# Preparing expert weights piece by piece between the steps of a two-layer mixture-of-experts stage

## The chip, the cores and the metric

The kernel runs on one core of one Trainium2 chip. The metric is the device time of one launch in microseconds, the median of the runs shown. Engines are named as in the profile: PE (TensorE), DVE (VectorE), ACT (ScalarE), POOL (GpSimd) and SP (SyncE, whose queue issues the loads).

## What is computed

Attention with a threshold, a gated MLP, and a soft mixture of eight experts, all in float32. The change touches the last part only:

```
logits = x @ w_gate                          # x: 2304 x 512, 8 experts
P = exp(logits - logits.max())
for _ in range(8):                           # Sinkhorn
    P /= P.sum(1, keepdims=True) + 1e-09
    P /= P.sum(0, keepdims=True) + 1e-09
    P *= N / E
for e in range(E):                           # w1: 512 x 1024, w2: 1024 x 512 for each expert
    h = np.maximum(x @ w1[e], 0.0)
    out += P[:, e:e + 1] * (h @ w2[e])
```

## The kernel before

**Work.** Every float32 matrix is held as two float16 parts (a high part and the remainder), and a product takes three passes. In the last part each expert is cut into two halves of 512 hidden columns, so there are 16 half experts (`h` = 0 to 15, `NE`), and the tokens into three groups (`NGR`). A half expert and a group make a unit `u` (48 units). Within a unit a block scheme with seven products (`ORDER`, `SECOND`) replaces the eight of a 2 x 2 block product, for x·w1 (`first_step`, L894) and for h·w2 (`second_step`, L966).

**PE's order.** It is written out by hand (`manual_schedule`, L1023). The loop at L1024 goes over steps `k`; each has one first step (six matmuls of 384 columns, into the PSUM tiles `X` or `Z`; two chains of seven first steps for a unit), and after step 20 one or two second steps (six matmuls of 256 columns, into `P` or `Q`), three for every two `k`. A unit is 14 first and 21 second steps; a half expert is 42 values of `k`. `P` has two PSUM banks, `Q` one (L1003). A second step accumulates onto the bank that the last-but-one left, so DVE must have taken the earlier result out of it (L992, `acc <- P` or `acc <- Q`, called an eviction here) before PE may write again.

**The other engines.** They run in the order that the scheduler gives them from the order of tracing and from its own estimate of times. In the steady part DVE has the evictions (L992), the sums `u <- Z,u` (L922, L931, L940) and the remainders `h <- u,h` (L889 for the operands 0, 1 and 2). ACT copies and clips (L920 to L941) and makes the high parts (L888). POOL builds the four remaining operands in eight instructions a chain (L943 to L946 and L889).

**The weights of the next half expert.** `load_w` (L720) loads 1 MB into the tile `raw` (L728, names `w1r`, `w2r`), takes the largest magnitude with two reductions on DVE (`w1m`, L731) and one maximum (L735), and forms three sums and one difference on POOL (L742 to L745, L749 to L752, names `w1s`, `w2s`). `prep_w` (L755) passes the maximum through a matmul with the identity (`w1mxp`, L131) and a reduction (L133), makes a scale of it in five small DVE instructions (L78 to L84), and then splits seven blocks into high part and remainder: `split` (L715) is one ACT copy (L717) and one DVE subtraction (L718) for a block. `raw` has one buffer, shared by w1 and w2. In the loop (L1044 to L1052) `load_w` is traced at the first step of a unit and `prep_w` ten steps later, w1 in the first unit of a half expert, w2 in the second. There is nothing that holds these instructions to a place among DVE's, ACT's or POOL's others.

**Loads of x.** Tiles `xo` (`load_x`, L777) have `XB` = 12 buffers; all loads go through SP's queue in order. For the first three units they are transposing loads in three pieces and are written back (`x2s`).

Of the kernel before, what the change touches and what calls it, by code (L numbers as in the profile page):

```python
# [7 lines left out]
F32 = mybir.dt.float32  # L8
# [11 lines left out]
def kernel(  # L20
# [29 lines left out]
    P = 128  # L50
# [498 lines left out]
    def mlp_out(j, tT, pool=None):  # L549
        if pool is not None:  # L550
            xf = pool.tile([P, KD, FH], F32, tag="raw", name="xf", bufs=1)
            xf = xf.rearrange("p k f -> p (k f)").rearrange("p (o d) -> p o d", d=HD)
            xh = pool.tile([P, NOP, HD], F32, tag="sums", name="xh")
            xh = xh.rearrange("p o d -> p (o d)").bitcast(F16)
            xh = xh.rearrange("p (o l d) -> p o l d", l=2, d=HD)
# [155 lines left out]
    KX = 4  # L711
    XB = 12
    UNITS = NE * NGR
# [5 lines left out]

    def load_w(which, h):  # L720

        e, f0 = h // 2, h % 2 * FH
        if which == 1:
            src = moe2_w1[e, :, f0 : f0 + FH]
        else:
            src = moe2_w2[e, f0 : f0 + FH, :]
        r = pb.tile([P, 4, 512], F32, tag="raw", name=f"w{which}r{h}", bufs=1)
        nc.sync.dma_start(out=r, in_=src.rearrange("(k p) f -> p k f", p=P))  # L728
        m = small([P, 2], f"w{which}m", bufs=2)
        for a in range(2):  # L730
            V.tensor_reduce(  # L731
                m[:, a : a + 1], r[:, 2 * a : 2 * a + 2], AX.XY, ALU.max,
                apply_absolute_value=True,
            )
        V.tensor_tensor(m[:, 0:1], m[:, 0:1], m[:, 1:2], ALU.max)  # L735
        sm = pb.tile([P, 7, HD], F32, tag="sums", name=f"w{which}s{h}")
        sm = sm[:, 0:6].rearrange("p (o k) f -> p o k f", o=3)
        q11, q12 = r[:, 0:2, 0:HF], r[:, 0:2, HF:]
        q21, q22 = r[:, 2:4, 0:HF], r[:, 2:4, HF:]
        if which == 1:  # L740
            a11, a21, a12, a22 = q11, q12, q21, q22
            G.tensor_tensor(sm[:, 0], a21, a22, ALU.add)  # L742
            G.tensor_tensor(a21, a11, a21, ALU.subtract)
            G.tensor_tensor(sm[:, 1], sm[:, 0], a11, ALU.subtract)
            G.tensor_tensor(sm[:, 2], a12, sm[:, 1], ALU.subtract)  # L745
            parts = (a11, a12, a22, a21)
        else:
            b11, b12, b21, b22 = q11, q12, q21, q22
            G.tensor_tensor(sm[:, 0], b12, b11, ALU.subtract)  # L749
            G.tensor_tensor(b12, b22, b12, ALU.subtract)  # L750
            G.tensor_tensor(sm[:, 1], b22, sm[:, 0], ALU.subtract)
            G.tensor_tensor(sm[:, 2], b21, sm[:, 1], ALU.subtract)  # L752
            parts = (b11, b12, b22, b21)
        return m, parts, sm

    def prep_w(which, h, loaded, pool, bufs=1):

        m, parts, sm = loaded
        w = pool.tile([P, NOP, 2, 2, HF], F16, tag=f"w{which}", name=f"w{which}_{h}", bufs=bufs)
        bits = 3 if which == 1 else 8  # L760
        s, inv = pow2_scale(all_max(m[:, 0:1], f"w{which}mx"), 1, bits, f"w{which}_{h % 3}")
        for o, a in enumerate((*parts, sm[:, 0], sm[:, 1], sm[:, 2])):
            split((w[:, o, 0], w[:, o, 1]), a, s[:, 0:1])
        return w, inv

# [4 lines left out]

    w1[0], inv1[0] = prep_w(1, 0, load_w(1, 0), pb)

# [112 lines left out]
    def operand(u, op, f, src, engine):  # L885

        t = pc.tile([P, 2, TW], F16, tag="h", name=f"h{u}_{op}_{f}", bufs=26)
        A.activation(t[:, 0], src, AF.Copy)  # L888
        engine.tensor_tensor(t[:, 1], src, t[:, 0], ALU.subtract)  # L889
        hs[u, op, f] = t  # L890
# [74 lines left out]
    def second_step(u, jj, j, pools):  # L965
# [50 lines left out]

    w2[0], inv2[0] = prep_w(2, 0, load_w(2, 0), pc, 2)
    BEHIND = 7
    steps = None
    held = {}  # L1020
    owed = []
    done = 0
    with tc.manual_schedule(engines={mybir.EngineType.PE}):  # L1023
        for k, (c, j) in enumerate(ahead):  # L1024
# [4 lines left out]
            if f == 1:  # L1029
                owed.append(u * NOP + j + XB)  # L1030
            if h > 0 or (f == 0 and j == 6):
                if h == 0:
                    logits(g)
                for t in owed:
# [18 lines left out]
            want = (k + 1 - 14 - BEHIND) * 3 // 2
# [52 lines left out]
```

## Time and profile before

| | us |
|---|---|
| median of 3 runs | 2411.78 |
| lowest and highest | 2406.57, 2448.46 |
| the profiled execution's own time | 2404.14 |
| its span, first to last instruction | 2402.3 |

The profile is of one execution. A line number stands for a line of the kernel; "idle before" is time in which the engine stood before that instruction, with what released it.

### The profile page before, as it was taken

What the parts mean: (1) busy time and instruction counts of PE and PEld (TensorE: products, weight loads), DVE (VectorE), ACT (ScalarE), POOL (GpSimd) and SP (SyncE); (2) the same over time, 40 slices, a digit from 0 to 9 for tenths busy, and PEclk for the clock granted to TensorE, in tenths of its full rate; (3) what the DMA queues carried; (4) which work ended last, traced back from release to release, by engine and by line L of the source; (5) the groups of instructions that cost most, each with busy time, mean ns of one, the idle gap of its engine ahead of it and who ended that gap; (6) DMA issues with size and microseconds to landing.
All of it is one profiled execution on the core that took longest, in us unless ns stands there. A gap on an engine that the chain in (4) does not pass through costs nothing.

```text
span 2402.3 us, 44050 instructions
## 1 busy us (share of the span) xinstructions
PE 2030.8 (85%) x16464; PEld 1476.9 (61%) x16464; DVE 1652.3 (69%) x3442; ACT 1333.0 (55%) x2786; POOL 1275.2 (53%) x1404
## 2 busy tenths in 40 slices
PE   1468889999999597978889788887888878888899
PEld 0245766767766365656666566665666656666677
DVE  6998777777443567676676766667666676666756
ACT  6877878877433454444454454544545445454553
POOL 1346665667433644555555555555555555555554
PEclk9769999999999798999999899998999989999999
DMA  9885878777371642333333333333333333333332
GB/s 262 206 180 118 166 136 167 152 137 136 61 178 45 158 124 84 104 101 110 105 103 104 101 110 104 102 102 105 110 104 103 102 104 110 103 102 101 96 99 80
DMA packets 372038, 286.80 MB, mean 119 GB/s; under 512 B 286064, under 2 KB 299504, under 8 KB 371824
## 3 DMA queue, kind: packets, MB, share of 16 engines
q1 hardware_dynamic: 371232, 283.97, 45.0%
q8 instruction: 129, 2.11, 0.4%
q14 instruction: 85, 0.70, 0.1%
q0 software_dynamic: 64, 0.00, 0.0%
q10 hardware_dynamic: 528, 0.02, 0.0%
HBM read 192.04 MB, written 21.23 MB: 89 GB/s over the span
## 4 chain that ended last, share of the span: by engine, by line
PE 51%; DVE 13%; DMA 7%; issue 2%; ACT 2%; POOL 1%; SPq 0%; DVEq 0%; ACTq 0%; POOLq 0%
PE X L910 13%; PE P L982 12%; PE Q L982 10%; PE Z L910 9%; DVE w L718 4%; PE gv L530 4%; DMA w1r<-in_moe_w_dram 3%; DMA w2r<-in_moe_w_dram 3%; PE x L561 2%; DVE h L889 2%; DVE acc L992 2%; ACT w L717 1%; DVE w1m L731 1%; DVE w2m L731 1%; DMA eT<-hl 1%
## 5 line engine op out<-in xcount | busy, mean ns | idle before, releaser
L982 PEld LDWEIGHTS <-h 128*128 128x128 f16 x6048 | 607.4, 101 | 301.5 <-issue 155.9
L910 PEld LDWEIGHTS <-w 128*128 128x128 f16 x4032 | 406.2, 101 | 272.6 <-issue 88.2
L910 PE MATMUL X<-xo,w 128*128 128x384 f16 x2304 | 466.6, 342 | 53.9 <-ACT u2c L927 7.4
L982 PE MATMUL P<-w,h 128*128 128x256 f16 x3456 | 483.1, 281 | 20.5 <-DVE acc L992 13.9
L982 PE MATMUL Q<-w,h 128*128 128x256 f16 x2592 | 370.4, 282 | 115.3 <-DVE acc L992 112.8
L992 DVE SCALAR_TENSOR_TENSOR acc<-P,coef,acc 128x256 f32<-128x256 f32 x540 | 258.7, 479 | 143.7 <-PE P L982 140.9
L910 PE MATMUL Z<-xo,w 128*128 128x384 f16 x1728 | 333.2, 330 | 0.0
L992 DVE SCALAR_TENSOR_TENSOR acc<-Q,coef,acc 128x256 f32<-128x256 f32 x405 | 194.1, 479 | 149.7 <-PE Q L982 147.6
L304 POOL TENSOR_TENSOR hl<-e,hl 128x512 f16<-128x512 f32 x144 | 171.7, 1193 | 228.3 <-ACT hl L303 150.2
L530 PE MATMUL gv<-xnT,wg 128*128 128x256 f16 x1296 | 167.7, 278 | 10.2 <-DVE u L540 7.9
L530 PE MATMUL gv<-xnT,wv 128*128 128x256 f16 x1296 | 167.6, 275 | 0.0
L561 PE MATMUL x<-wo,tT 128*128 128x512 f16 x648 | 144.4, 379 | 1.1 <-DVE u L540 0.9
L330 PE MATMUL pv<-vs,eT 128*128 128x64 f16 (+1 forms) x2240 | 103.2, 201 | 49.9 <-DMA eT<-hl 45.3
L530 PEld LDWEIGHTS <-wg 128*128 128x128 f16 x1296 | 126.4, 99 | 30.1 <-issue 10.7
L330 PEld LDWEIGHTS <-eT 128*128 128x128 f16 (+1 forms) x2240 | 91.0, 106 | 76.8 <-DMA eT<-hl 59.3
L298 DVE SCALAR_TENSOR_TENSOR e<-S,nt,e 128x576 f32<-128x576 f32 x144 | 116.5, 810 | 30.8 <-ACT e L296 30.4
L530 PEld LDWEIGHTS <-wv 128*128 128x128 f16 x1296 | 126.4, 99 | 15.7 <-issue 0.2
L292 DVE TENSOR_REDUCE nt<-S 128x1 f32<-128x576 f32 x144 | 107.0, 751 | 31.2 <-PE S L282 30.6
L296 ACT ACTIVATE e<-S,nt,c 128x576 f32<-128x576 f32 x144 | 117.9, 820 | 0.3 <-issue 0.3
L545 POOL TENSOR_TENSOR tT<-u,tT 128x256 f16<-128x256 f32 x108 | 74.2, 687 | 74.6 <-ACT tT L544 74.6
L303 ACT ACTIVATE hl<-e 128x576 f16<-128x576 f32 x144 | 97.1, 676 | 17.3 <-DVE e L298 10.2
L561 PEld LDWEIGHTS <-tT 128*128 128x128 f16 x648 | 62.2, 98 | 71.8 <-issue 1.2
(2636 smaller groups left out, 3665.3 us busy)
## 6 DMA issues: line engine op xcount, KB each, us to landing
xo<-x2s SPq DMA_DIRECT2D x315, 384.0 KB, 3.0
w1r<-in_moe_w_dram SPq DMA_DIRECT2D x16, 1024.0 KB, 5.0
w2r<-in_moe_w_dram SPq DMA_DIRECT2D x16, 1024.0 KB, 5.3
x2s<-xo SPq DMA_DIRECT2D x21, 384.0 KB, 2.7
wgatew<-in_moe_w_gate_dram SPq DMA_DIRECT2D x12, 512.0 KB, 6.0
wo<-in_moe_w_out_dram SPq DMA_DIRECT2D x12, 512.0 KB, 4.2
wvalw<-in_moe_w_val_dram SPq DMA_DIRECT2D x12, 512.0 KB, 4.4
x2d<-xs SPq DMA_DIRECT2D x24, 256.0 KB, 2.5
```

The costliest lines, as they stand in the source:

```text
L292: V.tensor_reduce(mx, sv, AX.XY, ALU.max)
L296: A.activation(ev, sv, AF.Exp, bias=nt[:, 0:1], scale=st["c2"][:, c : c + 1])
L298: V.scalar_tensor_tensor(ev, sv, nt[:, 1:2], ev, ALU.is_ge, ALU.mult, accum_out=sums[:, slot : slot + 1])
L303: A.activation(hl[:, 0:S], e, AF.Copy)
L304: G.tensor_tensor(hl[:, S + REM :], e[:, 0 : NCH * P], hl[:, 0 : NCH * P], ALU.subtract)
L330: T.matmul(o, lhsT=a, rhs=r, start=n == 0, stop=n == len(mm) - 1)
L530: T.matmul(gv[:, a, :], lhsT=w[:, l, kk, f * P : (f + 1) * P], rhs=xt[:, r * KD + kk, :], start=n == 0, stop=n == 3 * KD - 1,)
L561: T.matmul(ps, lhsT=tT[f][:, l, o : o + P], rhs=wo[:, f, r, :], start=n == 0, stop=n == 3 * KF - 1,)
L718: V.scalar_tensor_tensor(dst[1], src, s, dst[0], ALU.mult, ALU.subtract)
L910: T.matmul(ps, lhsT=w[:, a, l, kk, f * P : (f + 1) * P], rhs=xb[:, r * 2 + kk, :], start=n == 0 and j in (0, 1, 3), stop=n == 5, skip_grou ...
L982: T.matmul(ps, lhsT=hs[u, ao, f][:, l, jj * P : (jj + 1) * P], rhs=w2[h][:, bo, r, f, :], start=n == 0 and j in (0, 1, 3), stop=n == 5, sk ...
L992: V.scalar_tensor_tensor(y, ps, coef[h][:, i : i + 1], y, ALU.mult, ALU.add)
```

## The change

`load_w` and `prep_w` become one generator, `weight`, that stops (`yield`) after the load, after each reduction, after the maximum, after the scale, after each of POOL's four sums and after each of the seven splits: 17 calls of `next` in all. Before the loop a table `due` gives each call a step `k`: `base` plus an entry of `AT`. For w1 of half expert `hn` the base is 42·(hn−1), for w2 it is 18 later; the first pair is 10 and 6 more late. `behind()` ties every instruction of a piece behind the instruction of the main work that was last traced on the same engine (`main`: the operand's ACT copy and its difference on DVE or POOL, and the eviction on DVE). SP has no such entry, so loads are not tied. `raw` gets a second buffer, and `XB` goes from 12 to 10 for the room. The weights of half expert 0 are both loaded and scaled before the last MLP block. During half expert 0, `load_x` may run as soon as the logits of its group are traced.

```diff
-            xf = pool.tile([P, KD, FH], F32, tag="raw", name="xf", bufs=1)
+            xf = pool.tile([P, KD, FH], F32, tag="raw", name="xf", bufs=2)
...
-    XB = 12
+    XB = 10
...
-    def load_w(which, h):
+    main = {}
+
+    @contextmanager
+    def behind():
+
+        with ExitStack() as es:
+            for ins in main.values():
+                es.enter_context(tc.issue_after(ins.ins))
+            yield
+
+    def weight(which, h, pool, bufs=1):
...
-        r = pb.tile([P, 4, 512], F32, tag="raw", name=f"w{which}r{h}", bufs=1)
+        r = pb.tile([P, 4, 512], F32, tag="raw", name=f"w{which}r{h}", bufs=2)
         nc.sync.dma_start(out=r, in_=src.rearrange("(k p) f -> p k f", p=P))
+        yield
...
+        for x in sums:
+            G.tensor_tensor(*x)
+            yield
+        w = pool().tile([P, NOP, 2, 2, HF], F16, tag=f"w{which}", name=f"w{which}_{h}", bufs=bufs)
         for o, a in enumerate((*parts, sm[:, 0], sm[:, 1], sm[:, 2])):
             split((w[:, o, 0], w[:, o, 1]), a, s[:, 0:1])
+            yield
...
+    AT = (0, 6, 7, 7, 9, 10, 11, 11, 12, 12, 13, 14, 15, 16, 17, 18, 19)
...
+    first_w2 = weight(2, 0, lambda: pc, 2)
+    for _ in range(5):
+        next(first_w2)
...
-        A.activation(t[:, 0], src, AF.Copy)
-        engine.tensor_tensor(t[:, 1], src, t[:, 0], ALU.subtract)
+        main["A"] = A.activation(t[:, 0], src, AF.Copy)
+        main[engine is V] = engine.tensor_tensor(t[:, 1], src, t[:, 0], ALU.subtract)
...
-            V.scalar_tensor_tensor(y, ps, coef[h][:, i : i + 1], y, ALU.mult, ALU.add)
+            main[True] = V.scalar_tensor_tensor(y, ps, coef[h][:, i : i + 1], y, ALU.mult, ALU.add)
...
+    due = {}
+    for hn in range(1, NE):
+        for which, base in ((1, 42 * (hn - 1) + 10 * (hn == 1)), (2, 42 * (hn - 1) + 18 + 6 * (hn == 1))):
+            n = weight(which, hn, (lambda p: lambda: p)(w1_pool(hn) if which == 1 else pc), which)
+            for x in AT:
+                due.setdefault(base + x, []).append(n)
...
-            un, hn = k // 14, k // 14 // NGR + 1
-            if hn < NE and k % 14 in (0, 10) and un % NGR < 2:
-                which = 1 + un % NGR
-                if k % 14 == 0:
-                    held[which] = load_w(which, hn)
-                elif which == 1:
-                    w1[hn], inv1[hn] = prep_w(1, hn, held[1], w1_pool(hn))
-                else:
-                    w2[hn], inv2[hn] = prep_w(2, hn, held[2], pc, 2)
+            for n in due.pop(k, ()):
+                with behind():
+                    next(n, None)
```

Three places show how the order moves. In the rows the names carry a number that grows with the order of tracing; `Z_1`, `Z_3` are Z tiles of steps 1 and 3, `Q_0_3` is the Q tile of step 3 of the first token block.

The first is DVE, the reductions of a w1 (here of half expert 7). Before, they stand right behind the last split of the w2 ahead of them:

```order
L718 SCALAR_TENSOR_TENSOR w_6_17353<-w2s_17096,w_0_s,w_6_17353 128x512
L931 TENSOR_TENSOR u33b<-Z_3_17344,u33b 128x384
L992 SCALAR_TENSOR_TENSOR acc_11683<-P_1_17424,coef,acc_11683 128x256
L731 TENSOR_REDUCE w1m<-w1r_17814 128x1
L922 TENSOR_TENSOR u34a<-Z_1_17460,u34a 128x384
L731 TENSOR_REDUCE w1m<-w1r_17814 128x1
L889 TENSOR_TENSOR h_2_1_17403<-u33b,h_2_1_17403 128x384
L992 SCALAR_TENSOR_TENSOR acc_11730<-Q_1_3_17472,coef,acc_11730 128x256
```

Now they stand five main instructions apart, and the maximum and the reduction of the identity matmul follow with one eviction between:

```order
L905 TENSOR_TENSOR h_1_0_17954<-u36d,h_1_0_17954 128x384
L739 TENSOR_REDUCE w1m<-w1r_17810 128x1
L1008 SCALAR_TENSOR_TENSOR acc_12315<-P_2_17877,coef,acc_12315 128x256
L938 TENSOR_TENSOR u37a<-Z_1_17973,u37a 128x384
L1008 SCALAR_TENSOR_TENSOR acc_12399<-P_0_17989,coef,acc_12399 128x256
L956 TENSOR_TENSOR u36c<-Z_3_17885,u36c 128x384
L1008 SCALAR_TENSOR_TENSOR acc_12399<-Q_0_1_18023,coef,acc_12399 128x256
L905 TENSOR_TENSOR h_0_1_17982<-u37a,h_0_1_17982 128x384
L739 TENSOR_REDUCE w1m<-w1r_17810 128x1
L1008 SCALAR_TENSOR_TENSOR acc_12399<-P_0_17989,coef,acc_12399 128x256
L744 TENSOR_TENSOR w1m<-w1m 128x1
L133 TENSOR_REDUCE w1mx<-w1mxp 128x1
```

In PE's order the matmul `w1mxp` now stands behind the first step that follows the second step whose result is evicted between the second reduction and L744.

The second is DVE, the splits of a w2. Before, seven splits in four runs with one eviction between the runs:

```order
L718 SCALAR_TENSOR_TENSOR w_6_17353<-w2r_17090,w_0_s,w_6_17353 128x512 x2
L992 SCALAR_TENSOR_TENSOR acc_11598<-P_0_17277,coef,acc_11598 128x256
L718 SCALAR_TENSOR_TENSOR w_6_17353<-w2r_17090,w_0_s,w_6_17353 128x512 x2
L992 SCALAR_TENSOR_TENSOR acc_11683<-P_1_17424,coef,acc_11683 128x256
L718 SCALAR_TENSOR_TENSOR w_6_17353<-w2s_17096,w_0_s,w_6_17353 128x512 x2
L992 SCALAR_TENSOR_TENSOR acc_11683<-Q_1_1_17432,coef,acc_11683 128x256
```

Now the first five of the seven (a sixth follows four rows on, the seventh after seven more):

```order
L718 SCALAR_TENSOR_TENSOR w_7_18614<-w2r_18290,w_1_s,w_7_18614 128x512
L1008 SCALAR_TENSOR_TENSOR acc_11811<-P_2_18624,coef,acc_11811 128x256
L905 TENSOR_TENSOR h_2_0_18659<-u40b,h_2_0_18659 128x384
L718 SCALAR_TENSOR_TENSOR w_7_18614<-w2r_18290,w_1_s,w_7_18614 128x512 x2
L1008 SCALAR_TENSOR_TENSOR acc_11765<-Q_2_3_18671,coef,acc_11765 128x256
L1008 SCALAR_TENSOR_TENSOR acc_11811<-P_2_18624,coef,acc_11811 128x256
L718 SCALAR_TENSOR_TENSOR w_7_18614<-w2r_18290,w_1_s,w_7_18614 128x512
L905 TENSOR_TENSOR h_1_0_18707<-u40d,h_1_0_18707 128x384
L938 TENSOR_TENSOR u41a<-Z_1_18726,u41a 128x384
L718 SCALAR_TENSOR_TENSOR w_7_18614<-w2s_18551,w_1_s,w_7_18614 128x512
L1008 SCALAR_TENSOR_TENSOR acc_11888<-P_0_18742,coef,acc_11888 128x256
```

The splits moved apart, by one to three main instructions, except for one pair.

The third is SP, the load of the same w1. Before, it stands among loads of x whose numbers are some 400 below its own:

```order
L794 DMA xo_1_17351<-x2s 128x1536
L794 DMA xo_4_17406<-x2s 128x1536
L728 DMA w1r_17814<-in_moe_w_dram 128x4x512
L794 DMA xo_2_17451<-x2s 128x1536
L794 DMA xo_5_17513<-x2s 128x1536
```

Now some 600 below:

```order
L810 DMA xo_4_17119<-x2s 128x1536
L810 DMA xo_2_17213<-x2s 128x1536
L735 DMA w1r_17810<-in_moe_w_dram 128x4x512
L810 DMA xo_5_17259<-x2s 128x1536
L810 DMA xo_6_17321<-x2s 128x1536
```

Before, the first reduction of that w1 stands next to a Z tile with the number 17460, so the load is issued hardly ahead of it; now it stands next to 17954, some 740 numbers (28 of the 42 steps of a half expert, which take 1103 numbers) behind the loads around it. From half expert 4 on the order of DVE repeats exactly from one half expert to the next.

## Rows read from the trace of the kernel before

**Rows 1.** The page: busy time and share of each engine; clock by slices.
```profile
PE 2030.8 (85%) x16464; PEld 1476.9 (61%) x16464; DVE 1652.3 (69%) x3442; ACT 1333.0 (55%) x2786; POOL 1275.2 (53%) x1404
...
PEclk9769999999999798999999899998999989999999
```
**Rows 2.** Windows: stretch, its length, busy us (instructions) by engine, clock, DMA, GB/s.
```profile
773.00:970.70 197.70, 141.10 (x1062) 96.42 (x1061) 130.04 (x282) 98.69 (x213) 105.57 (x103) 0.85 0.42 124
...
1170.69:1270.31 99.62, 86.89 (x632) 63.15 (x632) 69.57 (x134) 49.83 (x98) 55.77 (x57) 0.95 0.34 105
...
2271.22:2353.44 82.22, 82.22 (x633) 61.65 (x631) 49.27 (x100) 42.01 (x85) 45.09 (x49) 1.00 0.28 88
```
**Rows 3.** The chain that ended last, at 1165 and 2174 us: start, us, what.
```profile
1160.95 4.90 DMA w1r<-in_moe_w_dram
...
1170.69 1.44 PE Q L982 x6
...
2174.38 1.44 PE Q L982 x6
```
**Rows 4.** Timeline of PE there: start, us, instruction, [idle before <-releaser].
```profile
1160.80 1.14 PE L910 MATMUL X<-xo,w 128*128 128x384 f16 x6 [1.48 <-ACT u21b L930]
...
1170.69 1.44 PE L982 MATMUL Q<-w,h 128*128 128x256 f16 x6 [4.05 <-DVE acc L992]
1171.92 1.97 PE L910 MATMUL X<-xo,w 128*128 128x384 f16 x6
```
**Rows 5.** Timeline of DVE there.
```profile
1159.49 1.40 DVE L718 SCALAR_TENSOR_TENSOR w<-w2r,w_s,w 128x512 f16<-128x512 f32 x2
...
1165.88 1.22 DVE L731 TENSOR_REDUCE w1m<-w1r 128x1 f32<-128x1024 f32 x1 [1.09 <-DMA w1r<-in_moe_w_dram]
...
1168.61 1.63 DVE L889 TENSOR_TENSOR h<-u21b,h 128x384 f16<-128x384 f32 x1
1170.16 0.47 DVE L992 SCALAR_TENSOR_TENSOR acc<-Q,coef,acc 128x256 f32<-128x256 f32 x1
```
**Rows 6.** Waits of PE, 970 to 2265 us: total, times, longest.
```profile
PE Q L982 <- DVE acc L992: 112.8, 26, 6.1
```
**Rows 7.** Timeline of PE without any preparation, 2312 to 2315 us.
```profile
2312.50 0.82 PE L982 MATMUL Q<-w,h 128*128 128x256 f16 x6
2313.15 1.14 PE L910 MATMUL Z<-xo,w 128*128 128x384 f16 x6
2314.13 0.82 PE L982 MATMUL P<-w,h 128*128 128x256 f16 x6
```
**Rows 8.** Timeline of DVE there.
```profile
2311.35 0.48 DVE L992 SCALAR_TENSOR_TENSOR acc<-Q,coef,acc 128x256 f32<-128x256 f32 x1
2311.74 0.48 DVE L992 SCALAR_TENSOR_TENSOR acc<-P,coef,acc 128x256 f32<-128x256 f32 x1
2313.35 0.48 DVE L992 SCALAR_TENSOR_TENSOR acc<-Q,coef,acc 128x256 f32<-128x256 f32 x1 [1.13 <-PE Q L982]
```
**Rows 9.** Timeline of DVE and of POOL, splits beside POOL's work.
```profile
1119.37 2.64 DVE L718 SCALAR_TENSOR_TENSOR w<-w1r,w_s,w 128x512 f16<-128x512 f32 x2 [0.34 <-ACT w L717]
...
1119.22 0.92 POOL L889 TENSOR_TENSOR h<-u18s,h 128x384 f16<-128x384 f32 x1
1120.09 1.37 POOL L889 TENSOR_TENSOR h<-u18c,h 128x384 f16<-128x384 f32 x1
```
**Rows 10.** Timeline of PE, a shorter idle time and the clock behind it.
```profile
913.54 1.47 PE L910 MATMUL X<-xo,w 128*128 128x384 f16 x6 [2.34 <-ACT u7b L930]
```
**Rows 11.** Timeline of PE and SP's queue at the start of the last part.
```profile
788.64 0.29 PE L131 MATMUL w2mxp<-ident,w2m 128*128 128x128 bf16 x1 [11.51 <-DVE w2m L735]
...
805.33 0.29 PE L131 MATMUL w1mxp<-ident,w1m 128*128 128x128 bf16 x1 [10.45 <-DVE w1m L735]
...
825.03 4.96 PE L910 MATMUL X<-xo,w 128*128 128x384 f16 x18 [7.37 <-ACT u2c L927]
...
780.09 0.39 SPq L728 DMA_DIRECT2D w2r<-in_moe_w_dram  x1
```

More of the change, by code (lines that the diff above doesn't have):

```diff
@@ L1 @@
-from contextlib import ExitStack
+from contextlib import ExitStack, contextmanager
 import concourse.bass as bass
@@ L718, in split @@
         V.scalar_tensor_tensor(dst[1], src, s, dst[0], ALU.mult, ALU.subtract)
-    def load_w(which, h):
-        e, f0 = h // 2, h % 2 * FH
-        if which == 1:
-            src = moe2_w1[e, :, f0 : f0 + FH]
-        else:
-            src = moe2_w2[e, f0 : f0 + FH, :]
-        r = pb.tile([P, 4, 512], F32, tag="raw", name=f"w{which}r{h}", bufs=1)
+    main = {}
[6 more added lines that the diff above has]
+    def weight(which, h, pool, bufs=1):
+        e, f0 = h // 2, h % 2 * FH
+        src = moe2_w1[e, :, f0 : f0 + FH] if which == 1 else moe2_w2[e, f0 : f0 + FH, :]
+        r = pb.tile([P, 4, 512], F32, tag="raw", name=f"w{which}r{h}", bufs=2)
         nc.sync.dma_start(out=r, in_=src.rearrange("(k p) f -> p k f", p=P))
+        yield
         m = small([P, 2], f"w{which}m", bufs=2)
@@ L734, in load_w @@
             )
+            yield
         V.tensor_tensor(m[:, 0:1], m[:, 0:1], m[:, 1:2], ALU.max)
+        yield
+        bits = 3 if which == 1 else 8
+        s, inv = pow2_scale(all_max(m[:, 0:1], f"w{which}mx"), 1, bits, f"w{which}_{h % 3}")
+        yield
         sm = pb.tile([P, 7, HD], F32, tag="sums", name=f"w{which}s{h}")
@@ L741, in load_w @@
             a11, a21, a12, a22 = q11, q12, q21, q22
[L742 to L745, printed above, removed]
+            sums = (
+                (sm[:, 0], a21, a22, ALU.add), (a21, a11, a21, ALU.subtract),
+                (sm[:, 1], sm[:, 0], a11, ALU.subtract), (sm[:, 2], a12, sm[:, 1], ALU.subtract),
+            )
             parts = (a11, a12, a22, a21)
@@ L748, in load_w @@
             b11, b12, b21, b22 = q11, q12, q21, q22
[L749 to L752, printed above, removed]
+            sums = (
+                (sm[:, 0], b12, b11, ALU.subtract), (b12, b22, b12, ALU.subtract),
+                (sm[:, 1], b22, sm[:, 0], ALU.subtract), (sm[:, 2], b21, sm[:, 1], ALU.subtract),
+            )
             parts = (b11, b12, b22, b21)
[L754 to L761, printed above, removed]
+        for x in sums:
+            G.tensor_tensor(*x)
+            yield
+        w = pool().tile([P, NOP, 2, 2, HF], F16, tag=f"w{which}", name=f"w{which}_{h}", bufs=bufs)
         for o, a in enumerate((*parts, sm[:, 0], sm[:, 1], sm[:, 2])):
             split((w[:, o, 0], w[:, o, 1]), a, s[:, 0:1])
-        return w, inv
+            yield
+        (w1, w2)[which - 1][h], (inv1, inv2)[which - 1][h] = w, inv
+    AT = (0, 6, 7, 7, 9, 10, 11, 11, 12, 12, 13, 14, 15, 16, 17, 18, 19)
     w1, w2, inv1, inv2 = {}, {}, {}, {}
@@ L769, in w1_pool @@
         return pb if h % 2 == 0 else pc
-    w1[0], inv1[0] = prep_w(1, 0, load_w(1, 0), pb)
+    for _ in weight(1, 0, lambda: pb):
+        pass
+    first_w2 = weight(2, 0, lambda: pc, 2)
+    for _ in range(5):
+        next(first_w2)
     ORDER = ((0, 0, 0), (1, 1, 1), (2, 5, 4), (3, 4, 2), (4, 3, 5), (5, 2, 6), (6, 6, 3))
@@ L1015 @@
     ahead = [(c, j) for c, j in ahead if c >= 0] + [(NCHAIN - 1, 5), (NCHAIN - 1, 6)]
-    w2[0], inv2[0] = prep_w(2, 0, load_w(2, 0), pc, 2)
+    for _ in first_w2:
+        pass
     BEHIND = 7
     steps = None
-    held = {}
+    due = {}
[4 more added lines that the diff above has]
+                due.setdefault(base + x, []).append(n)
     owed = []
+    gated = -1
     done = 0
@@ L1030 @@
                 owed.append(u * NOP + j + XB)
-            if h > 0 or (f == 0 and j == 6):
-                if h == 0:
-                    logits(g)
+            if h == 0 and f == 0 and j == 6:
+                logits(g)
+                gated = u
+            if h > 0 or gated >= k // 14:
                 for t in owed:
@@ L1043 @@
                     steps = None
-            un, hn = k // 14, k // 14 // NGR + 1
-            if hn < NE and k % 14 in (0, 10) and un % NGR < 2:
-                which = 1 + un % NGR
-                if k % 14 == 0:
-                    held[which] = load_w(which, hn)
-                elif which == 1:
-                    w1[hn], inv1[hn] = prep_w(1, hn, held[1], w1_pool(hn))
-                else:
-                    w2[hn], inv2[hn] = prep_w(2, hn, held[2], pc, 2)
+            for n in due.pop(k, ()):
+                with behind():
+                    next(n, None)
             want = (k + 1 - 14 - BEHIND) * 3 // 2
```

## Prediction

> **What bounds the kernel now.** I read the page first. PE is busy 85% of the span, the next engine, DVE, 69%, and the granted clock stands at 9 of 10 in most slices of the second half, where a kernel without pauses would show it full [rows 1]. So I compared stretches. Three units with the weights' preparation (one half expert, one period of the pattern) take 99.62 us with 632 matmuls; three units near the end, where no weights are left to prepare, take 82.22 us with 633, PE busy throughout at a clock of 1.00 [rows 2]. The first steps and second steps of a half expert are 252 + 378 = 630 matmuls, so 82.2 us is what PE needs. From one long wait to the same wait ten periods later are 2174.38 − 1170.69 = 1003.7 us [rows 3], a period of 100.4 in the mean. The preparation costs PE 18.2 us a period.
>
> The chain of waits says how: a DMA of w1, DVE's work behind it, and then PE's Q [rows 3]. On PE it is a pause of 1.48 us behind ACT, which copies seven blocks in a row, then one of 4.05 us for an eviction; after that the step takes 1.44 and 1.97 us where it took 0.82 and 1.14, which is PE's lower clock [rows 4]. On DVE the reduction of w1 stood first in the queue and waited for its load, and an eviction that PE needed lay four instructions behind it [rows 5]. From 970 to 2265 us there are 26 such waits with 112.8 us [rows 6]: 13 periods. Per period that is 8.7 us of these waits, 3 of the 1.48 us pauses, 1 of short ones, and 5 of lower clock (1.44 + 1.97 in place of 0.65 + 0.98, and one more slow step, twice): 17.7 of the 18.2.
>
> The start has its own loss. From 773 to 970.7 us, 74 first steps, 81 second steps and three groups of logits are done; at the undisturbed pace (0.98 and 0.65 us from start to start [rows 7], some 5 us for the logits) that is 130 us in place of 197.7 [rows 2]: 67 us lost, of which 11.51, 10.45 and 7.37 us in three pauses [rows 11].
>
> **The change part by part.** *Loads.* The load of a w moves some 28 steps ahead of its first reduction, over 50 us, where it lands 5 us after its issue [rows 3]. With two raw buffers it waits for the preparation before last. I count the DMA's part of the waits as gone. SP's queue holds the loads of x behind it; with ten buffers a tile of x is asked for 11 steps (21 us) before its use, so a hold of a few us costs nothing; this cover is gone at some 18 us.
>
> *Instructions.* None is added or removed. DVE has 69.57 us of work a period and 49.27 without preparation [rows 2], so 20.3 us of pieces. At PE's full pace it would be busy 85% of 82.2 us. On average it fits; what counts is where the pieces lie against evictions.
>
> *The slack of an eviction.* It starts 0.04 us after the modelled end of its second step and takes 0.48, and the next DVE instruction starts 0.40 after it [rows 7, 8]. A bank is written again at the earliest after one second and one first step, so an eviction may be late by 0.95 us.
>
> *The two maxima.* The second reduction of w1 now stands between the evictions of Q and P, and the matmul `w1mxp` behind the first step that follows P. From the end of Q DVE needs 0.04 + 0.40 (eviction) + 0.47 (difference) + 1.13 (reduction, from its 1.22 less the overlap [rows 5]) + 0.40 + 0.14 (maximum), and some 0.12 to PE: 2.7 us. PE is there after 0.65 + 0.98 − 0.17 = 1.5. A new wait of 1.2 us. For w2 the difference meets POOL's sum (0.7 instead of 0.47) and a second difference stands before the maximum (0.48): 3.0 us, while PE has only a first step to do, 0.8: 2.2 us. Before, neither matmul made PE wait in a steady period, so the lower bound is 0; the upper is 3 each.
>
> *The splits.* Alone, two take 1.40 us; beside POOL's instructions two took 2.64, and POOL's took 1.37 instead of 0.92 [rows 5, 9]. Each ended some 0.55 us after the POOL instruction then running, so the two engines took turns. The Trainium skill has this as a rule: the page GPSIMD Engine Reference, Key points, says that GpSimd shares its SBUF interfaces with VectorE and contends with instructions that have two SBUF inputs. It speaks against the change, for it spreads the splits over the time in which POOL works; the page gives no price, and the trace agrees with it in these rows. If the two did not share and each split took its free 0.66, the sum below would keep some 4 us a period instead of 10.9, which would give 2404 − 27 − 13 × 14 = 2195 us.
>
> In the w2 stretch POOL has the eight instructions of a chain and three sums without a pause. Between the eviction of Q's step 3 and that of the next block's first P stand five splits, three evictions and three differences or sums: 5 × 1.17 + 3 × 0.40 + 3 × 0.57 = 8.8 us. I take 1.17, nearer to 1.32 (half of 2.64) than to the free 0.66. The first split is ready 1.1 us after Q's end (ACT comes to it then), and the last eviction ends 0.5 later: 10.4 us. PE comes to that bank's next write after four first and six second steps from Q's start, 7.8, less the 0.82 of Q itself: 7.0. So 3.4 us of waiting, 0.7 of it at Q and 2.7 at P. For w1 the same walk, with the sums of POOL beside the first splits, gives 0.8 twice: 1.6 us. Bounds: at 0.66 each all of it lies in the slack, 0; at 1.32 each two more us a period.
>
> *The clock.* An idle time of 1.48 us left PE at its higher level [rows 4]; one of 2.34 was followed by a first step of 1.47 us [rows 10]. Of the waits above only the 2.7 is beyond 2.34; I add 2.5 us once. The 2.2 is between the rows; both ends go to the range.
>
> *ACT.* Its seven copies in a row are now single or in pairs or threes (2 us), below the two steps for which X can wait; the 1.48 us pauses go.
>
> **The sum.** A period: 1.2 + 1.6 (w1) + 2.2 + 3.4 + 2.5 (w2) = 10.9 us in place of 18.2: 7.3 saved, 13 times: 95 us. At the start the w2 of half expert 0 is loaded before the last MLP block, so the 11.51 us wait goes, where its load was issued only at 780.09 [rows 11]. The 10.45 mostly stays: the next w1 still stands in SP's queue behind twelve transposing loads, each over a microsecond. With half of the 7.37 and of the later waits there I take 27 us; bounds −10 (the preparation now lies beside the Sinkhorn iterations on DVE) and 55. Total 122. The profiled execution had 2404.1 us, the span and 1.8 around it, 0.3% below the median of the runs: 2404 − 122 = 2282 us.
>
> Bounds of the period: 0 to 16 us left instead of 10.9, so 13 × 18.2 to 13 × 2.2 saved.
>
> **Rivals.** *A: the pieces vanish in the slack.* DVE has 15% of the period free, and PE without preparation never waits [rows 2]. For it: the maxima never made PE wait before, and most of the evictions have more than 0.95 us. Against: five splits and three evictions without a free moment. With 3 us left a period: 13 × 15.2 + 40 = 238 saved, 2166 us.
>
> *B: the loss only changes its name.* DVE and POOL take turns at every split (1.32 us), both maxima cost 3, both are long enough for the lower clock. Some 16 us stay: 13 × 2.2 + 10 = 39 saved, 2365 us. That the tie to the last main instruction leaves the order as it was is excluded by the rows of the order.
>
> *C: slower.* Before, PE pauses at two places a weight and falls to its lower clock once. Now it pauses at three, spread over most of the period. If each of six pauses cost the lower clock, at 2.5 us, with 8.4 of waits, a period loses 23.4 us: 13 × 5.2 = 68 more; with nothing won at the start 2472, with the 27 us 2445. It decides if pauses of 0.8 to 1.2 us lower the clock; the 1.48 us ones before did not, so it needs that several close together do.
>
> **How the numbers follow.** Forecast 0.58, its own range 2220 to 2340; A 0.22; B 0.14; C 0.06. The range for 8 in 10 leaves out about half of A (0.10), the upper end of B (0.04) and C: 2160 to 2372. A measurement here tells about 2% from no change; 2% under 2411.8 is 2363. Forecast and A are faster, B lies on the line and gives a little more than half to "same". Faster 0.83, within 2% 0.11, slower 0.06.
>
> **What would show it.** The wait of Q for evictions falls from 112.8 us to about 30 to 45 for Q, with as much again at P and at the two `mxp` matmuls, which had none. The reductions wait for no DMA. Splits take 0.9 us or more in the mean. A period is near 93 us, and the clock in it above 0.95. The w2mxp at the start has no pause of 11 us. Wrong: periods at 85 us (A; then splits beside POOL cost PE nothing), at 98 (B), first steps of over 1.4 us at many places (C), or a PE waiting for `xo`.

## Result and the profile after

The changed kernel takes 2297.3 us (median of four runs, 2293.7 to 2307.9) where the kernel before took 2409.5: a ratio of 0.9545, 95% interval 0.950 to 0.959. It is faster. One run of the kernel before, 2448.5 us, was slow and is left out of the ratio. The prediction was 2282, its range 2160 to 2372. The profiled execution took 2293.7 us with a span of 2291.6, 110.7 less than before.

The page, its rows of busy time and clock, answering to [rows 1] (PEclk is the granted clock of 40 equal slices, in tenths of full speed):

```profile
PE 1989.1 (87%) x16464; PEld 1457.2 (64%) x16464; DVE 1670.3 (73%) x3442; ACT 1324.4 (58%) x2786; POOL 1310.4 (57%) x1404
...
PEclk9869999999999989899999999999999999999999
```

The windows (columns as in [rows 2]): twelve half experts in a row, then two single ones.

```profile
1010.92:2124.55 1113.63, 1018.04 (x7585) 745.46 (x7585) 844.93 (x1596) 590.32 (x1177) 694.43 (x672) 0.98 0.37 113
1940.12:2031.53 91.41, 83.47 (x632) 61.55 (x632) 70.40 (x133) 49.20 (x99) 57.96 (x56) 1.00 0.38 114
2031.53:2124.55 93.02, 85.08 (x633) 62.22 (x633) 70.50 (x133) 49.20 (x100) 57.98 (x56) 0.98 0.38 113
```

A period is 1113.63 / 12 = 92.8 us, where 100.2 stood before. PE's waits from 950 to 2260 us, in place of the 112.8 us at Q of [rows 6] (total, times, longest):

```profile
PE P L998 <- DVE acc L1008: 44.5, 27, 2.5
PE w2mxp L131 <- DVE w2m L744: 30.9, 13, 2.4
PE w1mxp L131 <- DVE w1m L744: 17.7, 13, 1.4
PE Q L998 <- DVE acc L1008: 11.4, 13, 0.9
```

Every period has the same five. On PE's timeline, one of each (columns as in [rows 4]), with the same pause at w2mxp once without and once with slow steps behind it (at the lower clock they take 1.49 and 2.10 us in place of 0.82 and 1.14):

```profile
1940.12 0.82 PE L998 MATMUL Q<-w,h 128*128 128x256 f16 x6 [0.88 <-DVE acc L1008]
...
1951.14 0.81 PE L998 MATMUL P<-w,h 128*128 128x256 f16 x6 [0.75 <-DVE acc L1008]
...
1967.05 0.23 PE L131 MATMUL w2mxp<-ident,w2m 128*128 128x128 bf16 x1 [2.37 <-DVE w2m L744]
1967.12 0.82 PE L998 MATMUL P<-w,h 128*128 128x256 f16 x6
...
1987.85 0.81 PE L998 MATMUL P<-w,h 128*128 128x256 f16 x6 [2.46 <-DVE acc L1008]
...
2018.41 0.23 PE L131 MATMUL w1mxp<-ident,w1m 128*128 128x128 bf16 x1 [1.36 <-DVE w1m L744]
...
2058.47 0.29 PE L131 MATMUL w2mxp<-ident,w2m 128*128 128x128 bf16 x1 [2.38 <-DVE w2m L744]
2058.55 1.49 PE L998 MATMUL P<-w,h 128*128 128x256 f16 x6
2059.83 2.10 PE L926 MATMUL Z<-xo,w 128*128 128x384 f16 x6
```

What stands ahead of the w2 maximum on DVE's timeline:

```profile
2055.56 1.19 DVE L905 TENSOR_TENSOR h<-u81b,h 128x384 f16<-128x384 f32 x1
2056.67 1.21 DVE L739 TENSOR_REDUCE w2m<-w2r 128x1 f32<-128x1024 f32 x1
2057.80 0.54 DVE L905 TENSOR_TENSOR h<-u81d,h 128x384 f16<-128x384 f32 x1
2058.27 0.15 DVE L744 TENSOR_TENSOR w2m<-w2m 128x1 f32<-128x1 f32 x1
```

and on POOL's, beside the first of these rows and beside the next ones shown:

```profile
2055.06 1.27 POOL L768 TENSOR_TENSOR w2s<-w2r 128x512 f32<-128x512 f32 x1
...
2073.34 1.58 POOL L768 TENSOR_TENSOR w2r<-w2r 128x512 f32<-128x512 f32 x1
2074.89 3.39 POOL L768 TENSOR_TENSOR w2s<-w2r,w2s 128x512 f32<-128x512 f32 x2
```

The reduction no longer waits for a DMA, but a difference of 0.54 us alone takes 1.19 beside POOL's sum, and PE is ready 2.4 us too early. On DVE again, what stands ahead of the 2.46 us wait of P that ends at 2080.88: two splits, which take 3.44 us beside three of POOL's sums, and later the eviction for which P waits:

```profile
2073.72 3.44 DVE L718 SCALAR_TENSOR_TENSOR w<-w2r,w_s,w 128x512 f16<-128x512 f32 x2
...
2080.35 0.47 DVE L1008 SCALAR_TENSOR_TENSOR acc<-P,coef,acc 128x256 f32<-128x256 f32 x1
```

The groups of splits on DVE, 950 to 2260 us (count, busy us, mean ns, then DVE's idle time before them and what ended it):

```profile
L718 DVE SCALAR_TENSOR_TENSOR w<-w2r,w_s,w 128x512 f16<-128x512 f32 x56 | 75.0, 1358 | 0.0
L718 DVE SCALAR_TENSOR_TENSOR w<-w1r,w_s,w 128x512 f16<-128x512 f32 x52 | 50.8, 977 | 7.6 <-ACT w L717 7.6
L718 DVE SCALAR_TENSOR_TENSOR w<-w2s,w_s,w 128x512 f16<-128x512 f32 x42 | 45.0, 1071 | 4.8 <-ACT w L717 4.5
L718 DVE SCALAR_TENSOR_TENSOR w<-w1s,w_s,w 128x512 f16<-128x512 f32 x39 | 36.6, 940 | 0.0
```

At the start, where [rows 11] had 11.51, 10.45 and 7.37 us, the last two remain, shorter:

```profile
799.69 4.00 PE L926 MATMUL X<-xo,w 128*128 128x384 f16 x12 [5.89 <-ACT u2c L943]
811.29 0.29 PE L131 MATMUL w1mxp<-ident,w1m 128*128 128x128 bf16 x1 [7.61 <-DVE w1m L744]
```

Where the 110.7 us came from, between the same matmuls of both traces (counted from the first X): up to the first X the change costs 2.9 us (772.7 in place of 769.8); from there to the first long steady wait of Q it wins 26.3 (238.2 in place of 264.5); the twelve periods behind it win 89.2 (1113.6 in place of 1202.8); from the last such Q to the end it loses 1.9 (167.1 in place of 165.2).

### The profile page after: what moved, and what is told of

Its sections match the earlier page's. It is cut to its first block, busy times and chain, and to the rows that moved or that the text cites. A ratio compares the mean times of both kernels' runs of the same rounds, so it can differ in the third digit from the quotient of the medians.

```text
span 2291.6 us, 43968 instructions
## 1 busy us (share of the span) xinstructions
PE 1989.1 (87%) x16464; PEld 1457.2 (64%) x16464; DVE 1670.3 (73%) x3442; ACT 1324.4 (58%) x2786; POOL 1310.4 (57%) x1404
## 4 chain that ended last, share of the span: by engine, by line
PE 51%; DVE 15%; POOL 3%; issue 3%; DMA 2%; ACT 1%; SPq 1%; DVEq 0%; POOLq 0%; ACTq 0%
PE P L998 14%; PE X L926 11%; PE Q L998 9%; PE Z L926 9%; DVE w L718 5%; PE gv L530 4%; DVE acc L1008 3%; DVE h L905 3%; PE x L561 2%; DVE w1m L739 1%; DVE w2m L739 1%; SPq L804 1%; DMA xo<-x2d 1%; ACT w L717 1%; DMA w1r<-in_moe_w_dram 1%
## 5 line engine op out<-in xcount | busy, mean ns | idle before, releaser
L998 PEld LDWEIGHTS <-h 128*128 128x128 f16 x6048 | 596.0, 99 | 221.3 <-issue 86.8
L926 PEld LDWEIGHTS <-w 128*128 128x128 f16 x4032 | 399.9, 99 | 211.6 <-issue 24.4
L998 PE MATMUL P<-w,h 128*128 128x256 f16 x3456 | 469.5, 275 | 55.7 <-DVE acc L1008 44.5
L926 PE MATMUL X<-xo,w 128*128 128x384 f16 x2304 | 440.1, 328 | 10.3 <-ACT u2c L943 5.9
L998 PE MATMUL Q<-w,h 128*128 128x256 f16 x2592 | 357.3, 275 | 12.2 <-DVE acc L1008 11.4
L926 PE MATMUL Z<-xo,w 128*128 128x384 f16 x1728 | 341.5, 336 | 0.0
```

The lines of the kernel that those rows point to most:

```text
L926: T.matmul(ps, lhsT=w[:, a, l, kk, f * P : (f + 1) * P], rhs=xb[:, r * 2 + kk, :], start=n == 0 and j in (0, 1, 3), stop=n == 5, skip_grou ...
L998: T.matmul(ps, lhsT=hs[u, ao, f][:, l, jj * P : (jj + 1) * P], rhs=w2[h][:, bo, r, f, :], start=n == 0 and j in (0, 1, 3), stop=n == 5, sk ...
```

## Experiments

Runs with one execution are read to some 15 us, the spread of the changed kernel's own four. Periods are taken from one steady wait or maximum to the same one eleven to thirteen half experts later. In the diffs the list AT has, in order: the load, two reductions, the maximum, the scale, four sums, seven splits, the end.

**1. The maximum two steps later.** Is the wait at the maxima one of order? The scale, and with it the matmul of the maximum, moves behind the second sum; the fields of the list change with it (two sums, the scale, two sums).

```diff
-    AT = (0, 6, 7, 7, 9, 10, 11, 11, 12, 12, 13, 14, 15, 16, 17, 18, 19)
+    AT = (0, 6, 7, 7, 10, 11, 11, 11, 12, 12, 13, 14, 15, 16, 17, 18, 19)
```

> The maximum over the partitions and the scale stand two of TensorE's first steps later (step 11 in place of 9, behind the second sum of POOL); everything else keeps its place. Theory, DVE's order: the matmuls w1mxp and w2mxp wait 1.36 and 2.37 us because the reduction and the differences ahead of them on DVE end too late; two steps are 3.9 us, so both waits go, and with them the slow steps behind w2mxp (1.4 us a period in the mean). A period falls from 92.8 to about 87.3 us, the time by 13 x 5.5 = 72 us to 2222 us; the wait of 2.46 us at P stays. Rival, the lost time only moves: the time that PE does not wait at the maxima it waits at the next evictions, P and Q grow by 3 to 4 us a period, and the time is 2275 to 2295 us.

2233.2 us. The waits at both maxima are gone; what is left (950 to 2260 us):

```profile
PE P L999 <- DVE acc L1009: 44.6, 28, 2.5
PE Q L999 <- DVE acc L1009: 17.9, 13, 1.4
```

A period is 88.7 us, 4.1 less, not 5.5: Q waits 1.38 in place of 0.88, and the slow steps, gone from w2mxp, now stand behind the 2.46 us pause of P in 9 of 14 cases. The theory holds, the sum was 11 us too good.

**2. No sums on POOL.**

```diff
         for x in sums:
-            G.tensor_tensor(*x)
+            if h == 0:
+                G.tensor_tensor(*x)
             yield
...
-        for o, a in enumerate((*parts, sm[:, 0], sm[:, 1], sm[:, 2])):
+        rest = (sm[:, 0], sm[:, 1], sm[:, 2]) if h == 0 else parts[:3]
+        for o, a in enumerate((*parts, *rest)):
```

> Leaves out POOL's four sums of each weight from half expert 1 on; the three splits that read a sum read a raw block instead, so DVE and ACT have the same instructions in the same order. Theory, DVE and POOL take turns: the splits (0.94 to 1.36 us in the mean) fall to 0.75 to 0.9, the pair of 3.4 us to about 1.4; the waits of P (2.46 and 0.75 us) and Q (0.88) all but go, 4 us a period and a little more: 2294 - 13 x 4.1 = 2240 us. The maxima wait as before (w2's a little less). Rival, DVE's order alone: five splits in a row of evictions are late whatever POOL does; P still waits some 2 us, and the time is 2280 to 2294 us.

2213.1 us, a period of 87.2. This kernel leaves the sums out and so shows only what they cost. DVE's instructions are the same; in each period one split of w2 and one eviction of Q have changed places, but the eviction for which P waited stands behind the same five splits as before. From the start of the first split to the start of that eviction it takes 6.77 us (from 1997.59) in place of 8.70 (from 2071.65 in the changed kernel). PE's waits:

```profile
PE w2mxp L131 <- DVE w2m L744: 23.4, 13, 1.8
PE w1mxp L131 <- DVE w1m L744: 17.7, 13, 1.4
PE P L1000 <- DVE acc L1010: 12.0, 27, 0.5
```

The 2.46 us wait is gone with POOL's sums, 0.5 is left; the rival falls. The splits fall from 1.10 to 0.95 us in the mean, not below 0.9, for POOL's chains are still there. It won 27 us more than expected: no slow step is left behind the pause at w2mxp, now 1.80 us, where they had cost some 18 us (1.4 a period), and the pause itself is 0.57 shorter, some 7 more.

**3. The start, and one raw buffer.** First the early w2 of half expert 0 alone undone (the first two lines of the edit), then the second buffer too, for the weights and for xf.

```diff
-    for _ in range(5):
-        next(first_w2)
...
-        r = pb.tile([P, 4, 512], F32, tag="raw", name=f"w{which}r{h}", bufs=2)
+        r = pb.tile([P, 4, 512], F32, tag="raw", name=f"w{which}r{h}", bufs=1)
```

> The load, the reductions and the scale of half expert 0's w2 stand behind the last MLP block again, as in the kernel before; the rest is the changed kernel. Theory: the start's gain of some 20 us comes from this early start alone; PE waits some 11 us at w2mxp near 790 us again, and the time is 2310 to 2318 us. Rival: the gain at the start comes from the second raw buffer and the later w1; then the time stays at 2292 to 2300 us.

> As the kernel with the late start, and one raw buffer in place of two; it is to be compared with that one. Theory, the order of the pieces does it: the last split that reads the raw tile stands three steps ahead of the next weight's load, and the reductions six steps behind the load (11 us, where it lands in 5 to 6), so no reduction waits for a DMA and the time is that of the late start within 8 us. Rival, the second buffer took the DMA waits away: the reductions wait 1 us and more for their load twice a period, evictions behind them are late, and the time is 25 to 60 us above the late start.

2299.0 and 2316.1 us. With two buffers and the late start the first w2 has no wait at all:

```profile
772.48 0.22 PE L131 MATMUL w2mxp<-ident,w2m 128*128 128x128 bf16 x1
```

With one buffer it is back, the wait of the first w1, 7.83 us in the run with two, is longer, and the next w2, which had none, waits too:

```profile
785.91 0.29 PE L131 MATMUL w2mxp<-ident,w2m 128*128 128x128 bf16 x1 [11.50 <-DVE w2m L744]
...
814.57 0.29 PE L131 MATMUL w1mxp<-ident,w1m 128*128 128x128 bf16 x1 [12.24 <-DVE w1m L744]
...
854.38 0.29 PE L131 MATMUL w2mxp<-ident,w2m 128*128 128x128 bf16 x1 [8.88 <-DVE w2m L744]
```

So with the second buffer the early call adds nothing: the theory of the first run falls, and the start's gain needs the buffer. In the steady part one buffer changes nothing (93.6 us a period in both, no wait of a reduction for a DMA): the theory of the second run misses at the start and holds behind it.

**4. The pieces in two lumps again**, with the change's buffers, loads and pins.

```diff
-    AT = (0, 6, 7, 7, 9, 10, 11, 11, 12, 12, 13, 14, 15, 16, 17, 18, 19)
+    AT = (0, 14, 14, 14, 24, 24, 24, 24, 24, 24, 24, 24, 24, 24, 24, 24, 24)
```

> The changed kernel, with its loads, buffers and pins, but each weight's pieces in two lumps as in the kernel before: both reductions and the maximum at step 14 behind the load, the scale, the four sums and the seven splits at step 24. It undoes the spreading alone. Theory, the order of the pieces: no reduction waits for a DMA, but two reductions in a row (2.3 us) and three splits in a row (2 to 3.5 us) lie ahead of evictions; PE waits for these at Q and P, 5 to 7 us a week point, with slow steps behind it; a period is near 97 us and the time 2335 to 2380 us. Rival, the loads: what the change won came from loads that have landed in time; then the lumps cost nothing and the time is 2285 to 2310 us.

2292.7 us, a period of 93.2: as good as the change. The theory falls: spreading the pieces won nothing on balance. It exchanged waits. With lumps no maximum waits, but ACT's seven copies in a row hold X, and P waits for a row of splits:

```profile
2093.94 1.56 PE L926 MATMUL X<-xo,w 128*128 128x384 f16 x6 [3.46 <-ACT u84c L943]
...
2100.07 0.81 PE L998 MATMUL P<-w,h 128*128 128x256 f16 x6 [1.04 <-DVE acc L1008]
```

**5. The load late, the pins away, the buffer alone.** What then took the DMA waits away? Three runs, with one edit each, in this order: the load at the step of the first reduction; the changed kernel without pins; the kernel before with two raw buffers (xf likewise), ten tiles of x and the changed kernel's rule of when these may be loaded.

```diff
-    AT = (0, 6, 7, 7, 9, 10, 11, 11, 12, 12, 13, 14, 15, 16, 17, 18, 19)
+    AT = (6, 6, 7, 7, 9, 10, 11, 11, 12, 12, 13, 14, 15, 16, 17, 18, 19)
...
-            for ins in main.values():
+            for ins in ():
...
-    XB = 12
+    XB = 10
...
-        r = pb.tile([P, 4, 512], F32, tag="raw", name=f"w{which}r{h}", bufs=1)
+        r = pb.tile([P, 4, 512], F32, tag="raw", name=f"w{which}r{h}", bufs=2)
```

> The changed kernel with each weight's load issued at the step of its first reduction (step 6 in place of 0); pins and pieces as they were. Theory, the pins: SP's queue runs some ten tiles of x ahead of TensorE, so a load still stands over 15 steps (30 us) ahead of the reduction that is pinned, lands in 6 us, and nothing waits: 2290 to 2302 us. Rival, the steps between load and reduction: DVE waits for the DMA again, evictions behind it are late, 4 us and slow steps twice a period: 2340 to 2400 us.

> The changed kernel without the pins: two raw buffers, the loads and the pieces at the same steps, but the scheduler may put a piece where it likes; on DVE the reductions move ahead of where the changed kernel has them, in pairs, and the splits stand in rows of three and four. Theory, the pins hold the reductions behind their loads: without them DVE waits for DMAs again and Q waits 4 us at a time; 2350 to 2410 us, near the kernel before. Rival, the second buffer and the early load: 2290 to 2310 us, as with the lumps.

> The kernel before with two raw buffers alone (and ten tiles of x, with the rule of when x may be loaded, to make room). Loads and reductions stand in the same call, so the scheduler puts the load on SP next to the reductions on DVE. Theory, the load has to be issued steps ahead of its reductions: DVE still waits for the DMA in the steady part, Q still waits 4 us twice a period, a period stays at 97 to 100 us; only the start is some 15 to 25 us shorter: 2365 to 2395 us. Rival, the second buffer alone lets the load go early enough: Q's long waits go, 2290 to 2330 us.

2291.0, 2276.2 and 2363.0 us. The late load costs nothing in sum (92.2 us a period, but 16.7 us of waiting for the first w1 in place of 7.6). It is not late in the trace: the pins hold the reductions back, and the load is still issued some 64 us ahead of the first of them, so a short distance was not tested by it. Without pins the time does not go back, it is 17 us better than the lowest run of the changed kernel (one run); the theory of the pins falls. DVE's waits for loads there, 950 to 2260 us:

```profile
DVE w1m L739 <- DMA w1r<-in_moe_w_dram: 5.8, 8, 2.2
DVE w2m L739 <- DMA w2r<-in_moe_w_dram: 3.0, 2, 2.3
```

With the second buffer alone they stay at 34 us, as before the change (34.8 from 970 to 2265 us), and so do Q's long waits (970 to 2265 us):

```profile
DVE w2m L731 <- DMA w2r<-in_moe_w_dram: 17.2, 12, 1.9
DVE w1m L731 <- DMA w1r<-in_moe_w_dram: 17.1, 12, 2.6
```

```profile
PE Q L982 <- DVE acc L992: 85.2, 25, 4.4
```

A period is 98.3 us, where the changed kernel and the runs of experiment 3, the lumps, the late load and the run without pins have 91.9 to 93.6. The distance between load and reduction is not what they have in common. From the issue of a load to the start of its first reduction there are 64 us in the changed kernel and 8.5 for w2 with one raw buffer, and no reduction waits; but without pins there are only 5.4 in the mean, as with the second buffer alone (5.3) and before (5.0 and 5.4), and the loads land after about 5. What that run has less of is waits for loads: 8.8 us in all in place of 34. Such a wait is passed on to PE, as the same place of two half experts shows in it:

```profile
1316.56 0.38 SPq L735 DMA_DIRECT2D w2r<-in_moe_w_dram  x1
1321.94 2.33 DVE L739 TENSOR_REDUCE w2m<-w2r 128x1 f32<-128x1024 f32 x2
1324.72 0.82 PE L998 MATMUL P<-w,h 128*128 128x256 f16 x6 [0.85 <-DVE acc L1008]
...
1408.12 0.38 SPq L735 DMA_DIRECT2D w2r<-in_moe_w_dram  x1
1415.17 2.34 DVE L739 TENSOR_REDUCE w2m<-w2r 128x1 f32<-128x1024 f32 x2 [2.33 <-DMA w2r<-in_moe_w_dram]
1417.96 0.81 PE L998 MATMUL P<-w,h 128*128 128x256 f16 x6 [2.92 <-DVE acc L1008]
```

The run without pins differs from the second buffer alone in other things too: X pauses once a period for 0.9 us, where it paused twice for 1.48, and reductions and splits lie elsewhere among the evictions. How much of the 6.4 us a period is the loads' and how much is the order's, no run separates. One buffer is enough for the steady gain where pins hold the reductions; what it does without pins was not tried.

**6. Every piece on a step of its own.** Sums as soon as POOL has ended a chain and the reductions are done, the scale six steps behind the maximum, seven splits over eleven steps. The fields of the lists are load, two reductions, maximum, four sums, scale, seven splits, end, with a list for w1 and one for w2, and the first half expert's bases are 7 and 25. The second run has the reductions three steps and the sums and the scale one step later, the third also the splits three steps later (of these two the list of w1 is shown; that of w2 moves alike).

```diff
-    AT = (0, 6, 7, 7, 9, 10, 11, 11, 12, 12, 13, 14, 15, 16, 17, 18, 19)
+    AT = {
+        1: (0, 9, 10, 10, 12, 12, 13, 13, 16, 19, 20, 21, 22, 27, 28, 29, 29),
+        2: (0, 12, 13, 13, 15, 15, 16, 16, 19, 22, 23, 24, 25, 30, 31, 32, 32),
+    }
...
+        1: (0, 12, 13, 13, 13, 13, 14, 14, 17, 19, 20, 21, 22, 27, 28, 29, 29),
...
+        1: (0, 12, 13, 13, 13, 13, 14, 14, 17, 22, 23, 24, 25, 30, 31, 32, 32),
```

> Every piece of a weight gets a step of its own over some 30 steps: the sums when POOL has ended a chain, the matmul of the maximum three and more steps behind the maximum, the seven splits at the steps in which POOL mostly has nothing of a chain to do (the steps 5, 6, 0, 1, and 6, 0, 1 of the blocks of seven). Theory: what is left in the changed kernel is pieces ahead of evictions and DVE and POOL taking turns; both go: no wait at the maxima, splits of 0.7 to 0.9 us, P and Q wait under 2 us a period; a period of 83.5 to 85.5 us, the time 2170 to 2205 us. Rival: a piece costs PE about the same wherever it stands; then only the maxima's waits go, as in the run with the maximum two steps later: 2225 to 2240 us.

> As the run with every piece on a step of its own, with the reductions and sums some steps later, so that the next run can share them: splits in the steps in which POOL is mostly idle. Theory: 2170 to 2210 us, splits of 0.7 to 0.9 us in the mean. Rival (a piece costs the same wherever it stands): 2225 to 2240 us.

> The run before with one edit: all splits stand three steps later, which is where POOL works on a chain (steps 1 to 4, and 2 to 4, of the blocks of seven). Same instructions, same spread, same sums. Theory, DVE and POOL take turns: the splits take 1.0 to 1.3 us in the mean, POOL's own work gets longer too, P and Q wait 3 to 5 us a period, and the time is 30 to 60 us above the quiet run. Rival, DVE's order alone: the splits are spread as before, so the two times agree within 8 us.

2145.9, 2192.4 and 2234.4 us, periods of 82.3, 85.8 and 89.0. The first beats both kernels, so it was timed:

> The kernel with every piece on a step of its own again, timed against the kernel before in five rounds: 2146 us, a ratio of 0.885 to 0.895; PE does not wait between 1000 and 1985 us.

2147.0 us, median of five; ratio to the kernel before 0.892, 95% interval 0.890 to 0.894, which is 0.892 / 0.9545 = 0.934 of the changed kernel. The window from 1000 to 1985 us and the splits of that run:

```profile
1000.00:1985.00 985.00, 985.00 (x7565) 739.01 (x7563) 804.39 (x1591) 586.84 (x1172) 705.16 (x670) 1.00 0.41 127
```

```profile
L718 DVE SCALAR_TENSOR_TENSOR w<-w2r,w_s,w 128x512 f16<-128x512 f32 x56 | 46.6, 833 | 2.6
L718 DVE SCALAR_TENSOR_TENSOR w<-w1r,w_s,w 128x512 f16<-128x512 f32 x52 | 46.6, 896 | 3.3 <-ACT w L717 3.3
```

PE is busy for all 985 us at the full clock: the preparation costs it nothing, with the same instructions, and DVE at 82%. The rival (a piece costs the same wherever it stands) falls.

The pair of the second and third run is inconclusive on its own question. The time differs by 42 us, as expected, but not for the reason given: the means of the splits are 0.86 and 0.93 us (over all four groups), for several of the splits that were to meet a chain stood in POOL's idle time and took 0.74. In the third run two splits fell together again, and POOL's first sum waited for the last split of the weight before (60.7 us in 13 periods), for the sums have one buffer. The first and the second run say more about order: their splits have the same mean, 0.86 us, only the reductions, the sums and the scale stand later, and that alone costs 3.5 us a period.

## Why the prediction was right, and where not

**The period.** Forecast 82.2 + 10.9 = 93.1 us, measured 92.8. Term by term: the w1 maximum 1.2, measured 1.36; the w2 maximum 2.2, measured 2.37; the w1 splits 0.8 at Q and 0.8 at P, measured 0.88 and 0.75; the w2 splits 0.7 at Q and 2.7 at P, measured below 0.2 and 2.46; the clock 2.5, measured about 1.4. The five splits, three evictions and three differences or sums that were put at 8.8 us take 8.70 in the trace. The waits sum to 7.8; each also costs the 0.17 us by which a step's modelled end runs into the next, and some waits under 0.3 us add the rest.

**The clock** was mis-sized and misplaced. I put it behind P's 2.7 us, since the 2.34 us pause of [rows 10] had lowered it; it came behind w2mxp, in 8 of 13 periods, and behind P's 2.46 in two of 14, there from the second step on. One of these two, behind the pause that ended at 1244.67:

```profile
1245.33 1.47 PE L926 MATMUL X<-xo,w 128*128 128x384 f16 x6
```

**The splits.** The sharing of DVE and POOL was taken from the rows [rows 5, 9], with a rule of the Trainium skill (page GPSIMD Engine Reference, Key points) beside them. The changed trace has 156 single splits to test it on. From its timelines of DVE and POOL, 950 to 2150 us: 53 single splits with nothing on POOL beside them took 0.73 to 0.74 us; 103 with a POOL instruction beside them took 1.12 in the mean, up to 1.55, and of the 90 that began while POOL was busy all but one ended 0.54 to 0.56 us behind the end of that POOL instruction. The differences of h do the same (0.54 to 0.56 alone, up to 1.46, ending 0.41 behind POOL). The 817 evictions, which have one input in PSUM, took 0.47 to 0.49 beside POOL or not, the reductions 1.20 to 1.21. The Trainium skill, page SBUF — State Buffer, section SBUF: two separate sides, calls this an exclusive lock: whichever starts first has the shared ports for its whole instruction, the other blocks. The trace agrees, for a blocked split still takes 0.55 of its 0.73 us behind POOL's end. Experiment 2 shows what it costs here: without the sums, P's 2.46 us fall to 0.5.

**The sum.** 13 × 7.3 = 95 for the periods: measured 7.4 a period, but twelve times. The thirteenth weight is the last; before, it had no next w1 behind it and so no long Q wait to lose, while the new waits at its maximum and at P came all the same: 1.9 us lost there. The count of 13 in that term was one too many. For the start 27 us were forecast, with 23.4 won up to the first steady Q, of which some 4.7 belong to the two thirds of a period behind my cut: about 19. So of the 11 us by which the sum was too good some 8 lie at the start and some 3 in the periods and the end. The step "the w2 of half expert 0 is loaded before the last MLP block, so the 11.51 us wait goes" names a part that was not needed: experiment 3 has no such wait without the early call, as long as there is the second raw buffer. Whether the early call would do it with one buffer was not run.

**Loads.** That the DMA's part of the waits goes was right, as was that a hold of SP costs nothing: no wait of PE for a tile of x stands in the trace. Of the rivals, A (2166 us, the pieces vanish in the slack) did not happen to this order of the pieces, but experiment 6 shows that its premise was sound: the slack is there. B and C did not happen; no pause of 0.7 to 1.4 us lowered the clock. Of the signs, 30 to 45 us of waiting at Q did not fit the prediction's own terms (0.8 and 0.7, 13 times: 20); 11.4 were measured.

**What the forecast never asked** is which part of the change the gain is from. The second buffer, with ten tiles of x and the rule for their loads, wins 42 us by itself (2405.1 to 2363.0: the start, and 1.9 a period). Everything else but the second buffer and the early w2 wins 93 (2409.5 to 2316.1); the buffer then adds 17, at the start. With the spreading undone, or the pins, the time is no worse. What the runs near 93 us a period share is that DVE waits little or not at all for loads, by whatever means; that this is the whole of the steady gain is not shown.

## What to carry to other kernels

An in-order engine that feeds a matmul engine has to be planned by what stands ahead of each eviction, not by its busy share: the same instructions cost 18, 10.6 or 0 us a period by their place alone. Leave a load the time to land before the first instruction that reads it (8.5 us from issue to read were always enough here, 5 were not), leave a result the time to arrive before the matmul that needs it, and give every other piece its own step, away from another engine's work on the same ports. Undo the parts one at a time before crediting any: here the time was no worse without the pins, or without the spreading, and the list of steps paid only when its numbers were chosen anew.

## What the runs showed of the hardware that was not expected

A pause of PE does not lower the clock at a sharp length. In the steady parts of all traces here every stretch of slow steps began within 1.4 us of the end of a pause. None of some 430 pauses of 0.6 to 1.8 us had one; of those of 2.36 to 2.5 us at w2mxp 38 of 54 did, of P's 2.46 us 24 of 70 (nine of 14 in experiment 1, none of 14 with the late load); of 2.8 to 2.9 us 11 of 14 (the run without pins); of X's 3.5 us 13 of 14 (the lumps); of the 50 at Q from 3.4 us on, all. For the same length the place counts, and the run, which no run here explains.

The block goes both ways: POOL's differences in a chain, 0.92 us alone, took 1.35 to 1.39 in 36 of 76 cases beside a split, and the sums 1.58 to 1.72 in place of 1.27 in all 65. Work on POOL slowed here just those DVE instructions that read SBUF twice, and no others.
